# Last keys' scores of two head pairs in quarters of the array, and a pair's preparation two pairs ahead

## The chip, the core and the metric

The kernel runs on one core of a Trainium2 chip. A core has a matrix engine (TensorE, PE in the profile), a vector engine (VectorE, DVE), an activation engine (ScalarE, ACT), a general engine (GpSimd, POOL) and an engine that here only issues transfers (SyncE, SP). Each engine works through its own queue of instructions in order, and waits for others at semaphores. The metric is the device time of one execution in microseconds (us). Weight loads of the matrix engine are shown apart as PEld.

## The reference

Sigmoid attention over 8 batches of 12 heads, 448 tokens and 64 columns a head, and behind it a two-layer network with 2048 hidden columns on every token:

```python
def _attn_ref(q, k, v):                     # q, k, v: (8, 12, 448, 64), float32
    S = q.shape[2]
    scale = 1.0 / np.sqrt(q.shape[-1])
    scores = scale * np.matmul(q, k.transpose(0, 1, 3, 2)) - np.log(S)
    attn = 1.0 / (1.0 + np.exp(-scores))
    return np.matmul(attn, v).astype(np.float32)

def _moe_ref(x, w_in, w_out):               # x: (3584, 768), w_in: (768, 2048), w_out: (2048, 768)
    h = x @ w_in
    g = np.where(h > 0.0, h, np.exp(np.minimum(h, 0.0)) - 1.0)
    return (g @ w_out).astype(np.float32)
```

Between the two the heads are put side by side: x = attn_out.transpose(0, 2, 1, 3).reshape(3584, 768).

## The kernel before

**Numbers.** Matmuls run in float16. Each operand is a sum of a high and a low part (`split`, L135: ACT writes high, DVE writes low), and each product takes three matmuls: high by high, low by high, high by low. The scales that go with it are powers of two, found from the largest row sums (`mx` on DVE, a matmul `pr` that sums over the partitions, then a short chain on DVE and POOL up to `sc`).

**Pairs.** The unit of attention is a pair of heads: two heads of 64 columns lie on the two halves of the 128 rows of the array. A batch has NP = 6 pairs, numbered hp = 0 to 5. The 448 keys are cut in NC = 3 tiles of 128 and a rest of R = 64, the last keys. For each tile `scores` (L382) takes six matmuls of 448 columns into `psc`, on alternate row halves. For the last keys it takes six 64*64 matmuls, where the heads lie on the diagonal of the array and both write one bank of `psc`. `soften` (L397) takes the sigmoid on ACT (`sg`, L401) and splits it into `at` (ACT L430, DVE L431), for the last keys into `ar` (ACT L420, DVE L422). `values` (L436) multiplies with the values into `pav`, on alternate column halves, and `finish` splits the result into `xh`.

**Preparation of a pair** has three steps. `prepare` (L307) takes `mx` of the raw q, k and v. Its `scales` sends the matmul `pr` and makes `sc`. Its third step, `transposed`, splits q and k into `nat` and v into `vn` (ACT and DVE), and sends a transposing DMA (L362, on SP's queue) that turns `nat` into `qk`, what `scores` reads. The raw inputs come by DMAs on SP (`load_qk`, `load_v`), with two buffers each.

**Stages.** Batch 0 is computed in float32, while `w_in` is converted. Then its first layer runs (`moe1`: 16 tiles `ph` of 18 matmuls, exp and max into `g`) while `w_out` is loaded and converted (`load_w_out`, L217). The order of this first part is found by a scheduler, from the dependences. From batch 1 on, PE, ACT, DVE and SP run in the order of the code. Attention of batch b is woven with the second layer of batch b-1: `moe2` comes as steps of three matmuls (`po`, L550, 48 matmuls a tile), which `fill(n)` puts between the attention's matmuls. There are 96 steps beside batches 1, 3, 5 and 7, and 128 beside 2, 4 and 6, shared out evenly over the six pairs. After a batch's last pair, `rescale` (L464) brings its `xh` to one scale (DVE L471), and `moe1` of the batch runs.

**One pair's order** in the code is: scores and sigmoid and split of tiles 0 and 1; the third step of the next pair's preparation and the loads of the pair three ahead; 5 steps of `fill` (8 in a batch's first pair); `mx` of the pair after next; scores, sigmoid and split of tile 2 and of the last keys; the rest of the pair's `fill`; `pr` and the scales of the pair after next; `values`; `finish`. So a pair's `qk` is issued while the pair before it runs. `psc` has two buffers (of two banks each), `sg` four, `at` three, `ar` one, `qk` and `vn` two, `nat` one.

## Time and profile before

| | |
|---|---|
| median of 3 runs | 1238.27 us (1235.75 to 1238.64) |
| profiled execution | 1238.24 us, of it 1236.5 us span |
| mean granted clock of TensorE | 0.984 |
| batch 0, its first layer, conversion of the weights | to about 165 us |
| attention of batch 1 with moe2 of batch 0 | about 165 to 260 us |
| later batches: attention of 3 (96 steps) | 77 us between 468 and 545 us |
| moe1 of one batch, without a gap | 51.09 us for 270 of its 288 matmuls |

The span is what the profiler saw from the first to the last instruction; what lies around it is 1.7 us. The page has a line for each engine's busy time, a strip of 40 slices, the chain of work that ended last, and groups of instructions by line. In a timeline row stand the start and length in us, the engine, the line, the operation, the tiles written and read, the shape (rows*columns of the array for matmuls), the number of instructions, and, in brackets, how long the engine stood idle before and what ended that.

### The profile page before, as it was taken

Reading aid. Unit: us, or ns where it says so; the run is one execution under the profiler, and the core shown is the slowest. Engines: PE = TensorE matmul, PEld = TensorE weight load, DVE = VectorE, ACT = ScalarE, POOL = GpSimd, SP = SyncE. Lnnn points to the kernel's source line nnn. Section 1 sums busy time; section 2 is a strip of 40 time slices with the busy share of each in tenths; the row PEclk is TensorE's granted clock in tenths of the full one; section 3 lists DMA queues with packets and bytes.
Section 4 is the critical chain, followed back from the end, with each engine's and each line's share of the span. In section 5 each row is a group of like instructions: output and inputs, shape, how many; then the busy total and the mean of one; then the engine's idle time right before and its main releaser. Section 6 shows DMA issues by size and latency. Waiting matters only on the chain.

```text
span 1236.5 us, 19394 instructions
## 1 busy us (share of the span) xinstructions
PE 1170.5 (95%) x7342; PEld 605.9 (49%) x7342; DVE 828.8 (67%) x1742; ACT 725.2 (59%) x1099; POOL 71.8 (6%) x275
## 2 busy tenths in 40 slices
PE   5869878999999999999999999999999999999998
PEld 2324434545455554555555554545455554555565
DVE  5897988875677647885677646885577745875500
ACT  5866788853766337864666537764576435873300
POOL 1021000000000000100010000010000000100000
PEclk9989988999999999999999999999999999999999
DMA  8946423420134203440144202440044301420000
GB/s 223 284 127 193 142 80 86 110 70 1 45 90 97 52 1 69 112 90 1 25 102 98 60 1 46 110 109 7 1 94 99 91 1 23 112 44 7 1 26 26
DMA packets 219549, 91.32 MB, mean 74 GB/s; under 512 B 183616, under 2 KB 215360, under 8 KB 219456
## 3 DMA queue, kind: packets, MB, share of 16 engines
q1 hardware_dynamic: 219456, 90.09, 29.6%
q8 instruction: 57, 0.93, 0.3%
q14 instruction: 36, 0.29, 0.1%
HBM read 59.77 MB, written 11.01 MB: 57 GB/s over the span
## 4 chain that ended last, share of the span: by engine, by line
PE 78%; DVE 8%; ACT 7%; DMA 3%; issue 2%; SPq 1%; POOL 0%; DVEq 0%; ACTq 0%
PE ph L520 32%; PE po L550 26%; PE psc L390 8%; PE pav L453 7%; PE po_r L550 5%; ACT sg L401 2%; DMA stage<-in_moe_w_in_dram 2%; ACT at L430 1%; DVE mx L140 1%; DMA wo<-in_moe_w_out_dram 1%; ACT L401 1%; DVE at L431 1%; DVE nat L137 1%; DVE ar L422 1%; DVE e L535 1%
## 5 line engine op out<-in xcount | busy, mean ns | idle before, releaser
L520 PE MATMUL ph<-xh,wi 128*128 128x448 f16 x2304 | 443.5, 354 | 7.1 <-DVE xh L471 4.2
L550 PE MATMUL po<-wo,g 128*128 128x384 f16 x2304 | 392.7, 328 | 0.0
L550 PEld LDWEIGHTS <-g 128*128 128x128 f16 x2688 | 256.5, 98 | 197.5 <-issue 35.2
L520 PEld LDWEIGHTS <-wi 128*128 128x128 f16 x2304 | 225.7, 98 | 221.2 <-issue 11.1
L532 ACT ACTIVATE e<-ph,msc 128x448 f32<-128x448 f32 x128 | 80.9, 633 | 210.7 <-PE ph L520 210.6
L431 DVE SCALAR_TENSOR_TENSOR at<-sg,at 128x896 f16<-128x896 f32 x126 | 137.3, 1090 | 82.5 <-ACT at L430 82.5
L401 ACT ACTIVATE sg<-psc,bias,sc 128x896 f32<-128x896 f32 (+1 forms) x168 | 166.6, 992 | 1.5
L534 DVE TENSOR_SCALAR e<-e 128x448 f32<-128x448 f32 x128 | 50.3, 394 | 171.4 <-ACT e L532 171.4
L390 PE MATMUL psc<-qk 64*128 64x448 f16 x1008 | 117.8, 356 | 12.5 <-ACT sg L401 12.5
L430 ACT ACTIVATE at<-sg 128x896 f16<-128x896 f32 x126 | 119.6, 950 | 4.0
L136 ACT ACTIVATE xh<-pav,sc 128x448 f16<-128x448 f32 x48 | 30.4, 634 | 131.5 <-PE pav L453 129.8
L136 ACT ACTIVATE g<-e,msc 128x384 f16<-128x384 f32 (+1 forms) x192 | 95.9, 533 | 8.0 <-DVE e L535 5.7
L137 DVE SCALAR_TENSOR_TENSOR g<-e,msc,g 128x384 f16<-128x384 f32 (+1 forms) x192 | 94.6, 522 | 1.9 <-ACT g L136 1.5
L535 DVE SCALAR_TENSOR_TENSOR e<-ph,msc,e 128x448 f32<-128x448 f32 x128 | 87.5, 683 | 4.0
L390 PEld LDWEIGHTS <-qk 64*128 64x128 f16 x1008 | 41.9, 97 | 81.3 <-issue 58.9
L453 PE MATMUL pav<-at,vn 128*64 128x448 f16 x756 | 79.5, 355 | 0.0
L453 PEld LDWEIGHTS <-vn 128*64 128x64 f16 x924 | 48.8, 109 | 46.6 <-issue 18.5
L550 PE MATMUL po_r<-wo,g 128*128 128x384 f16 x384 | 64.8, 326 | 0.0
L334 POOL TENSOR_SCALAR sc<-pw 128x1 f32<-128x1 f32 x42 | 11.8, 281 | 833.1 <-DVE pw L103 632.1
L137 DVE SCALAR_TENSOR_TENSOR nat<-raw,sc,nat 128x384 f16<-128x384 f32 (+1 forms) x126 | 59.1, 523 | 0.0
L136 ACT ACTIVATE nat<-raw,sc 128x384 f16<-128x384 f32 (+1 forms) x126 | 58.8, 528 | 0.0
L558 DVE TENSOR_SCALAR o<-po,osc 128x384 f32<-128x384 f32 x48 | 29.6, 617 | 41.5 <-PE po L550 35.8
(105 smaller groups left out, 857.7 us busy)
## 6 DMA issues: line engine op xcount, KB each, us to landing
stage<-in_moe_w_in_dram SPq DMA_DIRECT2D x16, 768.0 KB, 6.6
raw<-in_q_dram SPq DMA_DIRECT2D x96, 96.0 KB, 3.2
raw<-in_k_dram SPq DMA_DIRECT2D x96, 96.0 KB, 2.8
rv<-in_v_dram SPq DMA_DIRECT2D x48, 192.0 KB, 2.8
out_dram<-o SPq DMA_DIRECT2D x48, 192.0 KB, 2.1
wo<-in_moe_w_out_dram SPq DMA_DIRECT2D x19, 384.0 KB, 3.9
so<-in_moe_w_out_dram SPq DMA_DIRECT2D x13, 384.0 KB, 4.1
rv<-in_v_dram SPq DMA_DIRECT2D x96, 32.0 KB, 2.5
```

Of the source, the lines that this page charges most:

```text
L136: nc.scalar.mul(hi, src, s)
L137: nc.vector.scalar_tensor_tensor(lo, src, s, hi, op0=ALU.mult, op1=ALU.subtract)
L390: nc.tensor.matmul(psc[:, j, :S] if g < NC else psc[rows[j], 0, :S], kk[rows[j], o], qq[rows[j], :S], start=(n == 0), stop=(n == len(parts ...
L401: a = nc.scalar.activation(sg[:, :nb], psc[:, :nb, :S], AF.Sigmoid, bias=bias, scale=self.s_scale)
L430: nc.scalar.mul(hi, sg, 2.0**ATOP)
L431: nc.vector.scalar_tensor_tensor(lo, sg, 2.0**ATOP, hi, op0=ALU.mult, op1=ALU.subtract)
L453: nc.tensor.matmul(pav[rows[j], :S], vv[i][:, 2 * NC + j if g == NC else j * NC + g], sg[k][:, j], start=(g == 0 and n == 0), stop=(g == N ...
L520: nc.tensor.matmul(ph[:, :S], wi[:, wj, c, f * P : (f + 1) * P], xh[:, c, xj], start=(n == 0), stop=(n == 3 * NK - 1),)
L532: a = nc.scalar.activation(e, ph[:, :S], AF.Exp, scale=inv)
L534: nc.vector.tensor_scalar(e, e, 1.0, -1.0, op0=ALU.min, op1=ALU.add)
L535: nc.vector.scalar_tensor_tensor(e, ph[:, :S], inv, e, op0=ALU.mult, op1=ALU.max)
L550: nc.tensor.matmul(po[:, :HM], lh(gj, f), wo[:, i, f, wj], start=(n == 0), stop=(n == 3 * NF - 1),)
```

## The change

The diff does six things.

1. **Last keys of two pairs at once.** A new function `last_keys` takes the last keys' scores of an even pair hp and of the odd pair hp + 1 together, right after the even pair's tile 0. It has three groups of four 64*64 matmuls, one for each quarter of the array. The two heads of the even pair lie on one diagonal of it, those of the odd pair on the other; each pair has a bank of its own in the tile `pscr`. Two sigmoids of 448 columns, one for each pair, write `sgr`. The odd pair's `ar` is split at the end of the even pair's fill.
2. **Order of scores.** An even pair has tile 0 and the last keys ahead of the first fill, tiles 1 and 2 behind it. An odd pair has tiles 0 and 1 ahead of it and tile 2 behind. `soften` is cut in `sigmoid` and `parts`, and where two tiles are taken in a row in the odd pair, both sigmoids stand ahead of both splits.
3. **Preparation two pairs ahead.** Pair n makes scales, `nat`, `vn` and `qk` of pair n + 2, and `mx` of pair n + 3. `scales` with its `pr` matmul moves from the end of the pair to a place behind the first two steps of fill, and the third step moves behind the late scores. `qk` and `vn` have three buffers, `sc` five, `ar` two.
4. **Batch ends.** A batch's first pair (but for batch 1) prepares nothing. The preparation of the next batch's third pair stands in `moe1`, at hidden tiles 3 and 5 (`beside`).
5. **Fill.** The first pair of a batch has two steps more than its even share, and 11 steps ahead of the late scores where it had 8. `xh` has one buffer instead of two.
6. **Ahead of batch 1** the whole preparation of its second pair, the `mx` of its third and the loads of its fourth are made, where before the scales of the second and the loads of the third were.

The diff, cut to its core:

```diff
-            sc = sb.tile([P, n + 3], F32, tag="sc", name=f"sc{u}", bufs=3)
+            sc = sb.tile([P, n + 3], F32, tag="sc", name=f"sc{u}", bufs=5)
...
-            qk = sb.tile([P, 2, 2 * NC + 1, P], F16, tag="qk", name=f"qk{u}", bufs=2)
+            qk = sb.tile([P, 2, 2 * NC + 1, P], F16, tag="qk", name=f"qk{u}", bufs=3)
...
-            vn = sb.tile([P, 2, 2 * NC + 2, D], F16, tag="vn", name=f"vn{u}", bufs=2)
+            vn = sb.tile([P, 2, 2 * NC + 2, D], F16, tag="vn", name=f"vn{u}", bufs=3)
...
+        def soften(self, g):
+            nb = 2 if g < NC else 1
+            psc = self.psc.pop(g)
+            sg = sb.tile([P, 2, S], F32, tag="sg", name=f"sg{g}{self.u}", bufs=SB)
+            self.sigmoid(sg[:, :nb], psc[:, :nb, :S])
+            self.sg[g] = [sg]
+
+        def parts(self, g):
+
             if g == NC:
-                ar = sb.tile([P, 2, S], F16, tag="ar", name=f"ar{self.u}")
-                for j, r in enumerate(rows):
-                    nc.scalar.mul(ar[r, j], sg[r, 0], 2.0**ATOP)
+                (sg, i) = self.sg[g]
+                ar = sb.tile([P, 2, S], F16, tag="ar", name=f"ar{self.u}", bufs=2)
+                of = [rows[j ^ i] for j in range(2)]
+                for j, r in enumerate(of):
+                    nc.scalar.mul(ar[r, j], sg[r, i], 2.0**ATOP)
...
+    def last_keys(two):
+
+        psc = ps.tile([P, 2, 512], F32, tag="psc", name=f"pscr{two[0].u}", bufs=2)
+        o = slice(S, S + R)
+        for n in range(3):
+            for i, p in enumerate(two):
+                hi, lo = p.qk
+                kk, qq = [(hi, hi), (lo, hi), (hi, lo)][n]
+                for j in range(2):
+                    nc.tensor.matmul(
+                        psc[rows[j ^ i], i, :S], kk[rows[j], o], qq[rows[j], :S],
+                        start=(n == 0), stop=(n == 2),
+                    )
+        sg = sb.tile([P, 2, S], F32, tag="sg", name=f"sgr{two[0].u}", bufs=SB)
+        for i, p in enumerate(two):
+            p.sg[NC] = [sg, i]
+
+        def soften():
+            for i, p in enumerate(two):
+                p.sigmoid(sg[:, i], psc[:, i, :S])
+
+        return soften
...
-            xh_of[b] = sb.tile([P, NK, 2, S], F16, tag="xh", name=f"xh{b}", bufs=2)
...
     def pair_of(n):
         b, hp = pairs[n]
+        if hp == 0:
+            xh_of[b] = sb.tile([P, NK, 2, S], F16, tag="xh", name=f"xh{b}")
...
-    third = prepare_pair(EXACT * NP + 1)()
+    prepare_pair(EXACT * NP + 1)()()
     load_pair(EXACT * NP + 2)
+    load_pair(EXACT * NP + 3)
+    scales = prepare_pair(EXACT * NP + 2)
+    prepared = EXACT * NP + 2
...
+    def prepare_next():
+        nonlocal prepared, scales
+        load_pair(prepared + 2)
+        prepared += 1
+        scales = prepare_pair(prepared)
+
+    def beside(f):
+        nonlocal third
+        if f == 3:
+            third = scales()
+        if f == 5:
+            third()
+            prepare_next()
...
-                share = left // (NP - hp)
+                share = left // (NP - hp) + (2 if hp == 0 else 0)
                 tail = 4 if hp == NP - 1 else 0
-                p = pair_of(n)
-                for t in range(2):
+                works = hp > 0 or b == EXACT
+                if hp == 0:
+                    two = pair_of(b * NP), pair_of(b * NP + 1)
+                elif hp % 2 == 0:
+                    two = pair_of(b * NP + hp), pair_of(b * NP + hp + 1)
+                p = two[hp % 2]
+                p.scores(0)
+                if hp % 2 == 0:
+                    soften = last_keys(two)
+                    p.soften(0)
+                    soften()
+                    p.parts(0)
+                    early_ones, late_ones = (0,), (1, 2)
+                else:
+                    p.scores(1)
+                    p.soften(0)
+                    p.soften(1)
+                    p.parts(0)
+                    p.parts(1)
+                    early_ones, late_ones = (0, 1), (2,)
+
+                gap = 11 if hp == 0 else 5
+                fill(2)
+                if works:
+                    third = scales()
+                fill(gap - 2)
+                for t in late_ones:
                     p.scores(t)
+                for t in late_ones:
                     p.soften(t)
-                third()
...
+                    p.parts(t)
+                if hp % 2 == 0:
+                    p.parts(NC)
+                if works:
+                    third()
+                    prepare_next()
...
                 if hp == NP - 1:
-                    h = hidden(b)
+                    h = hidden(b, beside if b + 1 < B else None)
                     next(h)
                 fill(share - gap - tail)
-                third = second()
+                if hp % 2 == 0:
+                    two[1].parts(NC)
                 for t in range(NC + 1):
                     p.values(t)
                 p.finish()
```

Three places show what this does to the queues. The first is ACT's queue in the second pair (hp 1) of batch 2. `sg` is a sigmoid, `at` and `ar` are high parts of the sigmoids, `nat` and `vn` high parts of a later pair's q, k and v; the figure behind the tile's name is the pair or the key tile's pair. Before:

```order
L401 ACTIVATE sg_1_3276<-psc_1_3269,bias,sc_1_2592 128x896
L430 ACTIVATE at_1_3278<-sg_1_3276 128x896
L401 ACTIVATE sg_1_3288<-psc_1_3281,bias,sc_1_2592 128x896
L430 ACTIVATE at_1_3290<-sg_1_3288 128x896
L136 ACTIVATE nat_2_3293<-raw_2_2500,sc_2_3234 128x384
L136 ACTIVATE nat_2_3293<-raw_2_2500,sc_2_3234 128x128
L136 ACTIVATE nat_2_3293<-raw_2_2500,sc_2_3234 128x384
L136 ACTIVATE vn_2_3302<-rv_85,sc_2_3234 128x512
L401 ACTIVATE sg_1_3342<-psc_1_3335,bias,sc_1_2592 128x896
L430 ACTIVATE at_1_3344<-sg_1_3342 128x896
L401 ACTIVATE sg_1_3354<-psc_1_3347,bias,sc_1_2592 128x448
L420 ACTIVATE ar_1_3356<-sg_1_3354 64x448 x2
```

and now:

```order
L398 ACTIVATE sg_1_3322<-psc_1_3308,bias,sc_1_2535 128x896
L398 ACTIVATE sg_1_3324<-psc_1_3315,bias,sc_1_2535 128x896
L434 ACTIVATE at_1_3326<-sg_1_3322 128x896
L434 ACTIVATE at_1_3329<-sg_1_3324 128x896
L398 ACTIVATE sg_1_3369<-psc_1_3362,bias,sc_1_2535 128x896
L434 ACTIVATE at_1_3371<-sg_1_3369 128x896
L136 ACTIVATE nat_3_3374<-raw_3_2577,sc_3_3344 128x384
L136 ACTIVATE nat_3_3374<-raw_3_2577,sc_3_3344 128x128
L136 ACTIVATE nat_3_3374<-raw_3_2577,sc_3_3344 128x384
L136 ACTIVATE vn_3_3383<-rv_86,sc_3_3344 128x512
L136 ACTIVATE xh_3145<-pav_1_3453,sc_1_2535 128x448
```

The splits of `nat` and `vn` stand behind all three sigmoids and splits instead of behind two of them, and they are those of pair 3, not of pair 2. The sigmoid and `ar` of the last keys have left this pair.

The second place is DVE's queue in the third pair (hp 2) of batch 2, from its first split on. Before:

```order
L431 SCALAR_TENSOR_TENSOR at_2_3463<-sg_2_3461,at_2_3463 128x896
L431 SCALAR_TENSOR_TENSOR at_2_3475<-sg_2_3473,at_2_3475 128x896
L137 SCALAR_TENSOR_TENSOR nat_3_3478<-raw_3_3119,sc_3_3419,nat_3_3478 128x384
L137 SCALAR_TENSOR_TENSOR nat_3_3478<-raw_3_3119,sc_3_3419,nat_3_3478 128x128
L137 SCALAR_TENSOR_TENSOR nat_3_3478<-raw_3_3119,sc_3_3419,nat_3_3478 128x384
L137 SCALAR_TENSOR_TENSOR vn_3_3487<-rv_86,sc_3_3419,vn_3_3487 128x512
L140 TENSOR_REDUCE mx_4_3515<-rv_85 128x4
L140 TENSOR_REDUCE mx_4_3515<-raw_4_3305 128x7
L318 TENSOR_TENSOR mx_4_3515<-mx_4_3515,half 128x2
L431 SCALAR_TENSOR_TENSOR at_2_3529<-sg_2_3527,at_2_3529 128x896
L422 SCALAR_TENSOR_TENSOR ar_2_3541<-sg_2_3539,ar_2_3541 64x448 x2
L558 TENSOR_SCALAR o_2_0_3549<-po_2_0_3382,osc_1591 128x384
```

and now, from its second split on:

```order
L435 SCALAR_TENSOR_TENSOR at_2_3557<-sg_2_3555,at_2_3557 128x896
L435 SCALAR_TENSOR_TENSOR at_2_3562<-sg_2_3560,at_2_3562 128x896
L425 SCALAR_TENSOR_TENSOR ar_2_3565<-sgr_2_3499,ar_2_3565 64x448 x2
L137 SCALAR_TENSOR_TENSOR nat_4_3570<-raw_4_2858,sc_4_3519,nat_4_3570 128x384
L137 SCALAR_TENSOR_TENSOR nat_4_3570<-raw_4_2858,sc_4_3519,nat_4_3570 128x128
L137 SCALAR_TENSOR_TENSOR nat_4_3570<-raw_4_2858,sc_4_3519,nat_4_3570 128x384
L137 SCALAR_TENSOR_TENSOR vn_4_3579<-rv_85,sc_4_3519,vn_4_3579 128x512
L140 TENSOR_REDUCE mx_5_3592<-rv_86 128x4
L140 TENSOR_REDUCE mx_5_3592<-raw_5_3386 128x7
L318 TENSOR_TENSOR mx_5_3592<-mx_5_3592,half 128x2
L585 TENSOR_SCALAR o_r_3642<-po_r_3537,osc_1617 128x384
L425 SCALAR_TENSOR_TENSOR ar_3_3650<-sgr_2_3499,ar_3_3650 64x448 x2
```

All three splits of `at` and the pair's `ar` now stand ahead of `nat`, `vn` and `mx`, and a second `ar`, the odd pair's, behind them and behind the output tile `o`.

The third place is SP's queue around 100 us, ahead of the loads of `w_out` (L241), where `raw` and `rv` are loads of a pair's q, k and v. Before:

```order
L362 DMA_TRANSPOSE qk_0_805<-nat_0_798 128x14x128
L268 DMA raw_2_885<-in_q_dram 128x3x64 x2
L272 DMA raw_2_885<-in_q_dram 64x2x64
L268 DMA raw_2_885<-in_k_dram 128x3x64 x2
L272 DMA raw_2_885<-in_k_dram 64x2x64
L241 DMA wo<-in_moe_w_out_dram 128x384 x8
L241 DMA so_2_1346<-in_moe_w_out_dram 128x384
L241 DMA so_4_1383<-in_moe_w_out_dram 128x384
```

and now:

```order
L268 DMA raw_2_896<-in_q_dram 128x3x64 x2
L272 DMA raw_2_896<-in_q_dram 64x2x64
L268 DMA raw_2_896<-in_k_dram 128x3x64 x2
L272 DMA raw_2_896<-in_k_dram 64x2x64
L362 DMA_TRANSPOSE qk_1_891<-nat_1_884 128x14x128
L268 DMA raw_3_906<-in_q_dram 128x3x64 x2
L272 DMA raw_3_906<-in_q_dram 64x2x64
L268 DMA raw_3_906<-in_k_dram 128x3x64 x2
L272 DMA raw_3_906<-in_k_dram 64x2x64
L280 DMA rv_86<-in_v_dram 128x2x192
L285 DMA rv_86<-in_v_dram 64x2x64 x2
L241 DMA wo<-in_moe_w_out_dram 128x384 x8
```

A second transposing DMA and the loads of a further pair stand between the loads of `raw_2` and the first loads of `w_out`.

More of the change, by code (lines that the diff above doesn't have):

```diff
@@ L395, in scores, with sigmoid @@
             self.psc[g] = psc
-        def soften(self, g):
-            b, nb = self.b, 2 if g < NC else 1
-            psc = self.psc.pop(g)
-            sg = sb.tile([P, 2, S], F32, tag="sg", name=f"sg{g}{self.u}", bufs=SB)
-            a = nc.scalar.activation(
-                sg[:, :nb], psc[:, :nb, :S], AF.Sigmoid, bias=bias, scale=self.s_scale
-            )
-            if b - 1 in last_exp:
+        def sigmoid(self, to, psc):
+            a = nc.scalar.activation(to, psc, AF.Sigmoid, bias=bias, scale=self.s_scale)
+            if self.b - 1 in last_exp:
                 tc.add_manual_dep(
                     a.ins,
-                    last_exp[b - 1],
+                    last_exp[self.b - 1],
                     mybir.DependencyInfo(
@@ L412, in soften @@
                 )
-            if b < EXACT:
-                self.sg[g] = [sg]
-                return
-            if g == NC:
-                ar = sb.tile([P, 2, S], F16, tag="ar", name=f"ar{self.u}")
-                for j, r in enumerate(rows):
-                    nc.scalar.mul(ar[r, j], sg[r, 0], 2.0**ATOP)
-                for j, r in enumerate(rows):
+        def soften(self, g):
[5 more added lines that the diff above has]
+        def parts(self, g):
+            if g == NC:
+                (sg, i) = self.sg[g]
[3 more added lines that the diff above has]
+                    nc.scalar.mul(ar[r, j], sg[r, i], 2.0**ATOP)
+                for j, r in enumerate(of):
                     nc.vector.scalar_tensor_tensor(
-                        ar[rows[1 - j], j], sg[r, 0], 2.0**ATOP, ar[r, j],
+                        ar[of[1 - j], j], sg[r, i], 2.0**ATOP, ar[r, j],
                         op0=ALU.mult, op1=ALU.subtract,
@@ L427, in soften @@
                 return
+            (sg,) = self.sg[g]
             at = sb.tile([P, 2, 2, S], F16, tag="at", name=f"at{g}{self.u}", bufs=AB)
@@ L701, in attention_ffn @@
     of_moe2 = next(h)
+    def prepare_next():
[10 more added lines that the diff above has]
+            prepare_next()
+    third = None
     E = mybir.EngineType
@@ L718, in attention_ffn @@
             for hp in range(NP):
-                n = b * NP + hp
-                share = left // (NP - hp)
+                share = left // (NP - hp) + (2 if hp == 0 else 0)
                 tail = 4 if hp == NP - 1 else 0
-                p = pair_of(n)
-                for t in range(2):
+                works = hp > 0 or b == EXACT
[24 more added lines that the diff above has]
+                for t in late_ones:
                     p.scores(t)
+                for t in late_ones:
                     p.soften(t)
-                third()
-                if n + 3 < len(pairs):
-                    loaded[n + 3] = load_qk(*pairs[n + 3]), load_v(*pairs[n + 3])
-                gap = 8 if hp == 0 else 5
-                fill(gap)
-                second = prepare_pair(n + 2)
-                for t in range(2, NC + 1):
-                    p.scores(t)
-                    p.soften(t)
+                    p.parts(t)
[4 more added lines that the diff above has]
+                    prepare_next()
                 if b == EXACT and hp < NC:
```

## The prediction

> **What bounds the kernel now.** The page's first part gives each engine's busy time and its share of the span:
>
> ```profile
> PE 1170.5 (95%) x7342; PEld 605.9 (49%) x7342; DVE 828.8 (67%) x1742; ACT 725.2 (59%) x1099; POOL 71.8 (6%) x275
> ```
>
> TensorE is the bound, and the other two have room on average. An average hides stages, so I cut the span into stages (windows view; busy time of PE, PEld, DVE, ACT, POOL, then the clock). The first row is the expert layer after batch 2, the second the attention of batch 3:
>
> ```profile
> 408.00:468.00 60.00, 60.00 (x334) 30.95 (x331) 32.09 (x72) 20.86 (x34) 2.33 (x9) 1.00 0.06 16
> 468.00:545.00 77.00, 73.53 (x541) 38.32 (x539) 62.95 (x119) 62.38 (x85) 5.76 (x26) 1.00 0.45 99
> ```
>
> The expert layer has no gap, and the change leaves its matmuls alone. In attention PE stands idle for 3.5 of 77 us while DVE and ACT are over 80% busy. So the change can be worth two things: PE slots in attention, and the waits there. The waits of PE after 250 us (waits view: total, times, longest) are mostly these two:
>
> ```profile
> PE psc L390 <- ACT sg L401: 6.7, 6, 1.2
> PE pr L128 <- DVE mx L318: 6.6, 6, 1.1
> ```
>
> One ordinary pair of batch 3, PE's timeline (start, length, instructions):
>
> ```profile
> 519.88 1.31 PE L390 MATMUL psc<-qk 64*128 64x448 f16 x12
> 521.12 2.61 PE L550 MATMUL po<-wo,g 128*128 128x384 f16 x15
> 523.66 1.43 PE L390 MATMUL psc<-qk 64*128 64x448 f16 x12
> 525.02 5.54 PE L550 MATMUL po<-wo,g 128*128 128x384 f16 x33
> 530.39 0.17 PE L128 MATMUL pr<-mx,ones 128*128 128x12 bf16 x1
> 530.50 1.89 PE L453 MATMUL pav<-at,vn 128*64 128x448 f16 x18
> 532.22 0.55 PE L453 MATMUL pav<-ar,vn 128*64 128x448 f16 x4
> 532.70 1.31 PE L390 MATMUL psc<-qk 64*128 64x448 f16 x12
> 414.72 51.09 PE ph L520 x270
> ```
>
> The last row (chain of waits) sets the price of a 448-column slot: 51.09/270 = 0.189 us. The first twelve score matmuls take 521.12-519.88 = 1.24, that is six slots (1.135) and one change of the array's shape (0.105): two matmuls on the two halves of the rows share a slot. The second dozen holds the last keys' six 64*64 matmuls and takes 1.36: six slots and two changes. A pair lasts 12.82 us, without a wait. po's period is (5.37-0.10)/33, about 0.16. With 128 moe2 steps (batches 2, 4, 6) a pair has five or six steps more and lasts about 15.3.
>
> **Part 1, the quarters.** Two pairs spend six slots and two changes on last keys now. Afterwards, if four 64*64 quarters share a slot, three slots and one change: 3 x 0.189 + 0.10 = 0.66 us per two pairs, 21 times two pairs, **-13.9 us** (-1.98 a batch). If a quarter group takes two slots, 0.567 x 21 = 11.9 of it is lost. No row shows four at once, so the ends are 2 and 13.9. I take 13.9: two row halves into two banks, two column halves with different right sides (pav L453, 18 in 530.50 to 532.22, nine slots), and two quarters of one diagonal into one bank (the dozen at 523.66) all run side by side already.
>
> On that last point stands a rule against the change: the Trainium skill, page "TensorEngine Tiling (Array Packing)", section "Restrictions and Gotchas", says that different row tiles cannot use one PSUM bank at the same time. Each group of four puts both row halves into each bank. By the rule the sum would be 11.9 higher; but the old diagonal breaks it too and takes one slot in the trace, so it only gets a part of that rival's chance.
>
> **Part 2, waits that go.** Starts of a batch with 96 steps (470 on) and with 128 (324):
>
> ```profile
> 472.75 0.76 PE L390 MATMUL psc<-qk 64*64 64x448 f16 x6 [1.03 <-ACT sg L401]
> 478.64 0.17 PE L128 MATMUL pr<-mx,ones 128*128 128x12 bf16 x1 [1.13 <-DVE mx L318]
> 324.47 0.76 PE L390 MATMUL psc<-qk 64*64 64x448 f16 x6 [1.22 <-ACT sg L401]
> 542.49 0.17 PE L128 MATMUL pr<-mx,ones 128*128 128x12 bf16 x1 [1.06 <-DVE mx L318]
> 468.34 1.28 ACT L401 ACT_TABLE_LOAD   x1
> ```
>
> Behind the table load the first sigmoids come about 4 us after the first scores. In the first pair 33 po matmuls (5.4 us) now stand ahead of the second scores instead of 24, and its preparation is gone; both waits of that place go. With the short shape changes beside them (0.06 to 0.16 each, and 0.29 on ar) I count 4.28 us of waits in batches 3 and 5, 2.77 in batch 7 (no wait in its last pair), 1.28 in batches 2, 4 and 6, and 1.5 in batch 1 behind its start.
>
> **Part 3, waits that come.** ACT and DVE of the same ordinary pair, in the old order (T = 519.88):
>
> ```profile
> 520.66 1.10 ACT L401 ACTIVATE sg<-psc,bias,sc 128x896 f32<-128x896 f32 x1
> 524.62 1.40 ACT L136 ACTIVATE nat<-raw,sc 128x384 f16<-128x384 f32 x3
> 528.50 0.71 ACT L401 ACTIVATE sg<-psc,bias,sc 128x448 f32<-128x448 f32 x1
> 529.24 1.17 ACT L420 ACTIVATE ar<-sg 64x448 f16<-64x448 f32 x2
> 525.75 1.40 DVE L137 SCALAR_TENSOR_TENSOR nat<-raw,sc,nat 128x384 f16<-128x384 f32 x3
> 527.07 0.75 DVE L137 SCALAR_TENSOR_TENSOR vn<-rv,sc,vn 128x512 f16<-128x512 f32 x1
> 528.33 1.08 DVE L140 TENSOR_REDUCE mx<-raw 128x7 bf16<-128x896 f32 x1
> 530.64 1.27 DVE L422 SCALAR_TENSOR_TENSOR ar<-sg,ar 64x448 f16<-64x448 f32 x2
> DMA to landing us min/median/max: 4.0/4.0/4.4
> ```
>
> From T+0.78 ACT does sg, at, sg, at at 0.99 each and reaches nat at T+4.74; DVE ends nat at T+7.27, and the transposing DMA (last row) lands it 4.0 later, T+11.3. In the new odd pair a third sigmoid and split stand ahead: nat is 1.98 later, so it ends at about T+9.25 and **lands at T+13.3**. Formerly a whole pair lay between landing and use; now the next even pair's quarters want it right after its first scores. The second pair (15 steps) lasts 12.82 - 0.69 - 0.49 = 11.64, and six matmuls with a change are 0.67: wanted at T+12.3. So the third pair's quarters **wait 1.0**. In batches 2, 4 and 6 it is wanted at about T+15.2, and nothing waits.
>
> The quarters stand in PE's queue ahead of po, so the whole queue waits. In the third pair ACT has two short sigmoids (2 x 0.71) more ahead of its splits, so it reaches ar at 0.78 + 6 x 0.99 + 2 x 0.71 = T+8.1; ar, nat, vn, mx (0.68 + 1.08 + 0.17), o and the second ar then keep DVE until about T+16, 3.5 past the pair's end. The fourth pair's splits start some 1 us late on DVE, with at, at, the scale chain (1.03) and at ahead of nat: landing at about T+14.45 against 12.8 wanted, **1.65** in the fifth pair. The last pair has nat, vn and mx ahead of the rescaling of xh:
>
> ```profile
> 545.26 2.12 PE L550 MATMUL po<-wo,g 128*128 128x384 f16 x12
> 547.22 3.57 PE L520 MATMUL ph<-xh,wi 128*128 128x448 f16 x18
> 545.03 1.90 DVE L471 TENSOR_SCALAR xh<-xh,rr 128x896 f16<-128x896 f16 x5
> ```
>
> The first rescaled part is now ready at about T+12.4 with an idle DVE, T+14 with that lag, and ph wants it at T+12.13: 0.3 to 1.9. I take 1.9, since DVE's queue is filled, with 0.45 and 0.35 for the scale and pb around it. The first pair takes its 3 x 0.99 splits and two ars behind two more short sigmoids: pav waits about 0.95 for ar. The fourth pair's scale: 0 to 0.9, taken 0.3. Sum for batches 3 and 5: 0.95 + 1.0 + 0.3 + 1.65 + 2.7 = 6.6. Against 4.28 + 1.98 this is **+0.35 each**. Batch 7 prepares nothing at its end: 3.9 - 2.77 - 1.98 = **-0.85**. Batches 2, 4 and 6: -1.28 - 1.98 = **-3.26 each**.
>
> **Part 4, batch 1 and what is ahead of it.** SP's rows and DVE by stretch (windows):
>
> ```profile
> 99.98 1.24 SPq L285 DMA_DIRECT2D rv<-in_v_dram  x2
> 101.27 1.69 SPq L362 DMA_TRANSPOSE qk<-nat  x1
> 103.01 1.83 SPq L268 DMA_DIRECT2D raw<-in_q_dram  x2
> 107.59 4.48 SPq L241 DMA_DIRECT2D wo<-in_moe_w_out_dram  x8
> 102.20:107.20 5.00, 5.00 (x28) 2.60 (x27) 3.46 (x11) 2.51 (x4) 0.82 (x4) 1.00 0.73 148
> 107.20:112.20 5.00, 5.00 (x27) 2.39 (x26) 1.80 (x5) 1.72 (x4) 0.00 (x0) 1.00 0.86 221
> 112.20:119.50 7.30, 6.93 (x37) 3.11 (x36) 5.72 (x12) 6.43 (x14) 0.00 (x0) 1.00 1.02 395
> 176.53 0.48 PE L165 MATMUL so<-wo,ones 128*128 128x384 bf16 x1 [6.45 <-DVE wo L158]
> 197.02 1.30 PE L390 MATMUL psc<-qk 64*128 64x448 f16 x6 [4.22 <-ACT sg L401]
> ```
>
> A second transposing DMA (1.7) and the loads of a further pair's q, k (107.59 - 103.01 = 4.6) and v (1.24 and a third load, some 1.7) now stand ahead of the first w_out loads, so these start up to 8 later, and DVE, which bounds their conversion until 176, with them. DVE's idle time from 102 to 119.5 is 1.54 + 3.20 + 1.58 = 6.3, which takes the moved nat, vn, mx and scale chain (5.0). The delay lies between 0 and 8; I take 2.6. In batch 1 DVE also carries the rest of w_out, so the wait in the third pair lies between 1.0 and 1.0 + 4.2 (the row's wait): 3.8, in the fifth 2.5, at the end 2.7. With -1.5 and -1.98 this is +5.5, in all **+8.1**.
>
> **Sum:** -9.8 + 0.7 - 0.85 + 8.1 = -1.9 on the profiled execution's 1238.24 (the median is 1238.27): **1236.4 us**, no change; 0.3%, about what a measurement of this kernel can tell, is 3.7 us.
>
> **Rivals.** (a) **The waits for qk are shorter.** If the chain nat, transposing DMA, quarters is 1 us quicker than summed, because ACT runs ahead of DVE where I queued them, the waits of third and fifth pairs lose 2 in each of four batches: 1228. For it speaks the room on both engines, against it that every link is a row. Without any delay in batch 1: 1222. (b) **Slower: the chain is later.** Each us more costs 2 in each short batch, 8 in all; beyond 1.9 the long batches wait too. From 0.7 on the time is over 1242; at 1.0 it is 1244.4, at 1.5 about 1248. For it speaks that DVE is 82% busy in that stage and nat stands behind three more of its instructions. (c) **The quarters don't run four at once**, so the change doesn't do what it says: 1236.4 + 11.9 = 1248.
>
> **How the numbers follow.** The forecast, with its own range 1232 to 1242, has 0.36, (a) 0.36, (b) 0.18, (c) 0.10. Faster by over 0.3% (under 1234.5): 0.33 from (a) and 0.08 from the forecast's lower part, 0.41. Slower (over 1242): 0.14 from (b), 0.09 from (c), 0.23. The rest, 0.36, is within 0.3%. A range of 1225 to 1248 leaves out about 0.09 on either side.
>
> **What would show it.** Right: twelve 64*64 matmuls in about 0.6 us; no wait of psc for ACT in the first pairs; in batches 3 and 5 the third and fifth pairs' quarters wait 1 to 2 us behind the transposing DMA, with none in 2, 4 and 6; ph waits for xh; w_out loads start later. Wrong: quarters in 1.1 us, waits for qk in long batches or in none, or a stage that the sum leaves alone (the expert layer) longer than 51.09 per 270.

## The result and the profile after

| | before | changed |
|---|---|---|
| median | 1238.19 us (4 runs, 1235.75 to 1238.64) | 1247.13 us (4 runs, 1245.96 to 1248.09) |
| ratio to before | | 1.0076, 95% interval 1.0058 to 1.0093 |
| profiled execution | 1238.24 us | 1246.27 us |

The change makes the kernel slower by 0.8%, where no change was forecast. The engines' line of the page of the changed kernel:

```profile
PE 1162.9 (93%) x7342; PEld 599.5 (48%) x7342; DVE 828.8 (67%) x1742; ACT 722.4 (58%) x1099; POOL 95.2 (8%) x275
```

PE has 7.6 us less to do, and the span is longer: the saving is real and the waits outgrow it. To see where, the program is cut at its hidden layers (`ph`). An attention stage lasts from the last hidden matmul of one layer to the first of the next:

| stage | before | changed | forecast | measured |
|---|---|---|---|---|
| start of the program to the layer of batch 1 | 262.6 | 275.4 | +8.1 | +12.8 |
| attention of batches 2, 4, 6 | 3 x 94.1 | 90.9, 90.9, 91.1 | -9.8 | -9.5 |
| attention of batches 3 and 5 | 2 x 81.8 | 2 x 83.5 | +0.7 | +3.5 |
| attention of batch 7 | 80.1 | 81.0 | -0.85 | +0.9 |
| the layers of batches 1 to 7 | 7 x 54.35 | 3 x 54.52, 4 x 54.37 | 0 | +0.6 |
| sum | | | -1.9 | +8.3 |

The two profiled executions differ by 8.0; the rest is rounding and the program's end.

PE's timeline of the changed kernel in batch 3, the quarters and their neighbours:

```profile
475.43 0.74 PE L390 MATMUL psc<-qk 64*128 64x448 f16 x6
476.11 0.76 PE L477 MATMUL pscr<-qk 64*64 64x448 f16 x12
476.80 5.54 PE L577 MATMUL po<-wo,g 128*128 128x384 f16 x33
...
502.39 0.38 PE L477 MATMUL pscr<-qk 64*64 64x448 f16 x2
504.15 0.76 PE L477 MATMUL pscr<-qk 64*64 64x448 f16 x10 [1.38 <-DMA qk<-nat]
...
529.21 0.38 PE L477 MATMUL pscr<-qk 64*64 64x448 f16 x2
531.87 0.76 PE L477 MATMUL pscr<-qk 64*64 64x448 f16 x10 [2.29 <-DMA qk<-nat]
...
558.70 3.56 PE L547 MATMUL ph<-xh,wi 128*128 128x448 f16 x18 [2.25 <-DVE xh L498]
```

Twelve quarters take 476.80 - 476.11 = 0.69 us, three slots and a change: four run at once. In the third and fifth pairs the first two, on the even pair's own `qk`, start at once; the next needs the odd pair's `qk`, and PE stands for its transposing DMA. The two take a slot that four could share, and the ten behind the wait take 504.84 - 504.15 = 0.69 us, as twelve do. So the whole stretch from 502.39 to 504.15 is lost, 1.76 us, and 2.66 in the fifth pair. (The expectation of the quarters' experiment below takes a slot off each, 1.57 and 2.47.)

Why the `qk` is late stands in the odd pair ahead of it (hp 1 of batch 3), first in ACT's timeline, then in DVE's and POOL's:

```profile
495.77 0.95 ACT L434 ACTIVATE at<-sg 128x896 f16<-128x896 f32 x1
497.97 1.41 ACT L136 ACTIVATE nat<-raw,sc 128x384 f16<-128x384 f32 x3 [1.24 <-POOL sc L329]
```

```profile
493.79 2.09 DVE L435 SCALAR_TENSOR_TENSOR at<-sg,at 128x896 f16<-128x896 f32 x2 [1.07 <-ACT at L434]
496.41 0.17 DVE L328 RECIPROCAL sc<-pw 128x3 f32<-128x3 f32 x1
496.76 1.09 DVE L435 SCALAR_TENSOR_TENSOR at<-sg,at 128x896 f16<-128x896 f32 x1
498.62 1.42 DVE L137 SCALAR_TENSOR_TENSOR nat<-raw,sc,nat 128x384 f16<-128x384 f32 x3 [0.77 <-ACT nat L136]
```

```profile
496.89 1.05 POOL L329 TENSOR_SCALAR sc<-sc 128x3 f32<-128x3 f32 x1
```

ACT is ready for `nat` at 496.7, but `sc` isn't there. Its chain stands behind two splits of `at` on DVE (493.79) and leaves DVE at 496.6, and then POOL's step takes 1.05 us, beside DVE's third split of `at`. In the even pair, with DVE idle, the same step takes 0.23.

```profile
509.25 0.23 POOL L329 TENSOR_SCALAR sc<-sc 128x3 f32<-128x3 f32 x1
```

Over the whole execution POOL's 275 instructions take 95.2 us, where they took 71.8. The waits view of the whole execution has ACT's wait 19 times, the third row; it was in no list before, where the scales were made a pair earlier:

```profile
PE pscr L477 <- DMA qk<-nat: 14.8, 8, 2.8
PE ph L547 <- DVE xh L498: 11.0, 4, 4.2
ACT nat L136 <- POOL sc L329: 27.8, 19, 2.6
```

The start. SP's, ACT's, DVE's and PE's timelines of the changed kernel: the first loads of w_out, the first work on them, and the last matmul on w_out's magnitudes (`so`); the last row is that matmul in the kernel before:

```profile
106.91 1.53 SPq L362 DMA_TRANSPOSE qk<-nat  x1
114.97 4.68 SPq L241 DMA_DIRECT2D wo<-in_moe_w_out_dram  x8
```

```profile
119.26 0.55 ACT L153 ACTIVATE wo<-wo 128x384 f32<-128x384 f32 x1 [4.23 <-DMA wo<-in_moe_w_out_dram]
120.27 0.56 DVE L158 SCALAR_TENSOR_TENSOR wo<-wo 128x384 uint32<-128x384 uint32 x1 [4.02 <-ACT wo L157]
```

```profile
187.04 0.48 PE L165 MATMUL so<-to,ones 128*128 128x384 bf16 x1 [0.30 <-DVE to L158]
```

```profile
178.70 0.48 PE L165 MATMUL so<-to,ones 128*128 128x384 bf16 x1 [0.69 <-DVE to L158]
```

The loads start 7.4 us later than at 107.59, and the conversion ends 8.3 later. (Here and below, `so` ends where its last matmul starts, and a pair where its last matmul into `pav` starts.) The second pair of batch 1 ends at 218.0 instead of 209.4, 8.6 later. On ACT's queue behind `so` lie the last splits of w_out, in turn with DVE's, and that pair's first sigmoids come only behind them:

```profile
200.39 1.15 ACT L136 ACTIVATE wo<-wo,swo 128x384 f16<-128x384 f32 x2 [1.92 <-DVE wo L137]
204.29 1.15 ACT L136 ACTIVATE wo<-wo,swo 128x384 f16<-128x384 f32 x2 [0.15 <-DVE wo L137]
207.05 2.07 ACT L398 ACTIVATE sg<-psc,bias,sc 128x896 f32<-128x896 f32 x2
```

### The profile page after: what moved, and what is told of

Its sections match the earlier page's. It is cut to its first block, busy times and chain, and to the rows that moved or that the text cites. A ratio compares the mean times of both kernels' runs of the same rounds, so it can differ in the third digit from the quotient of the medians.

```text
span 1244.5 us, 19369 instructions
## 1 busy us (share of the span) xinstructions
PE 1162.9 (93%) x7342; PEld 599.5 (48%) x7342; DVE 828.8 (67%) x1742; ACT 722.4 (58%) x1099; POOL 95.2 (8%) x275
## 4 chain that ended last, share of the span: by engine, by line
PE 69%; DVE 12%; ACT 7%; DMA 6%; issue 2%; SPq 2%; POOL 1%; DVEq 0%; ACTq 0%
PE ph L547 31%; PE po L577 22%; PE po_r L577 5%; PE pav L457 5%; PE psc L390 5%; DMA qk<-nat 3%; ACT sg L398 2%; DVE at L435 2%; DMA stage<-in_moe_w_in_dram 2%; DVE mx L140 2%; DVE nat L137 1%; DVE ar L425 1%; PE pscr L477 1%; ACT at L434 1%; DMA wo<-in_moe_w_out_dram 1%
## 5 line engine op out<-in xcount | busy, mean ns | idle before, releaser
L398 ACT ACTIVATE sg<-psc,bias,sc 128x896 f32<-128x896 f32 x126 | 135.5, 1092 | 18.9 <-PE psc L390 16.7
L390 PE MATMUL psc<-qk 64*128 64x448 f16 x756 | 87.4, 353 | 4.1 <-ACT sg L398 4.1
L457 PE MATMUL pav<-at,vn 128*64 128x448 f16 x756 | 80.3, 358 | 0.0
L390 PEld LDWEIGHTS <-qk 64*128 64x128 f16 x756 | 30.2, 94 | 52.8 <-issue 33.9
```

The lines of the kernel that those rows point to most:

```text
L390: nc.tensor.matmul(psc[:, j, :S] if g < NC else psc[rows[j], 0, :S], kk[rows[j], o], qq[rows[j], :S], start=(n == 0), stop=(n == len(parts ...
L398: a = nc.scalar.activation(to, psc, AF.Sigmoid, bias=bias, scale=self.s_scale)
L457: nc.tensor.matmul(pav[rows[j], :S], vv[i][:, 2 * NC + j if g == NC else j * NC + g], sg[k][:, j], start=(g == 0 and n == 0), stop=(g == N ...
```

## The experiments

All are edits of the changed kernel or of one built on it. The time before, on the chips of these runs, had medians of 1236.1 to 1236.7 us, where it was 1238.2 beside the changed kernel's 1247.13. So differences from the changed kernel are uncertain by some 2 us, and the ratios to the time before on the same chip decide.

### The loads of batch 1's fourth pair behind eight w_out loads

```diff
-    load_pair(EXACT * NP + 3)
...
         if f >= 2:
             step(W_OUT)
+        if f == 8:
+            load_pair(EXACT * NP + 3)
```

> Edit to the changed kernel (1247.1): the loads of the fourth pair of batch 1 are issued behind the first eight w_out loads instead of ahead of them. Theory A (SP's queue: the first w_out load is issued at 114.97 instead of 107.59, DVE then stands idle 4.0 us in 116 to 120): these loads start about 6.5 us earlier, the first layer of batch 0 (80.3 us, 73.4 before) shortens by 4 to 6 us, and the time is 1241 to 1243. Theory B (DVE is bound by the moved work, nat, vn, mx and the scale chain of two pairs, 5 us): the loads start earlier, but the layer shortens by 1.5 us at most: 1245.6 or more.

1246.06 us (1245.20 to 1251.49), ratio 1.0090, interval 1.0067 to 1.0112. The first layer of batch 0 fell from 80.3 to 73.9 us, as by A, but the time hardly moved, as by B. `so` ends at 184.3 instead of 187.0 and the second pair at 215.8: of the 6.4 us that the layer gained, 2.2 are left behind the conversion. So it isn't the layer's length that sets the end there; the end of the conversion fits better. The profiled execution is the longest of the four, with a low granted clock behind several waits (last section).

### The quarters behind the first fill

```diff
-                if hp % 2 == 0:
-                    soften = last_keys(two)
-                    p.soften(0)
-                    soften()
-                    p.parts(0)
-                    early_ones, late_ones = (0,), (1, 2)
-                else:
-                    p.scores(1)
...
+                p.scores(1)
...
+                late_ones = (2,)
...
+                if hp % 2 == 0:
+                    soften = last_keys(two)
                 for t in late_ones:
                     p.scores(t)
+                if hp % 2 == 0:
+                    soften()
```

> Edit to the changed kernel (1247.1): an even pair takes tiles 0 and 1 ahead of its first fill, as an odd pair does, and the quarters and tile 2 behind it, 2.5 us or more later on PE. Theory A (the quarters stand in PE's queue ahead of everything and wait for the transposing DMA: 1.57 and 2.47 us of lost time in each of batches 3, 5 and 7, 1.24 and 2.98 in batch 1): all these waits go, 3 x 4.0 + 4.2 = 16 us, 1231; batches 2, 4 and 6 stay at 90.87. Theory B (the wait is only moved: ar comes later and pav waits for it, or DVE is so full that the pair's end waits instead): a quarter to a half of it comes back as waits of pav on ar, 1235 to 1240. Theory C (the lost time is not these waits): 1246 or more.

1222.08 us (1221.78 to 1222.40), ratio 0.9887, interval 0.9872 to 0.9901: some 23 us under the changed kernel by the two ratios (25 by the medians), more than A's 16. PE's timeline in the third pair of batch 3, and the waits view behind 250 us:

```profile
494.92 1.31 PE L390 MATMUL psc<-qk 64*128 64x448 f16 x12
496.16 1.15 PE L577 MATMUL po<-wo,g 128*128 128x384 f16 x6
497.15 0.17 PE L128 MATMUL pr<-mx,ones 128*128 128x12 bf16 x1
497.18 1.62 PE L577 MATMUL po<-wo,g 128*128 128x384 f16 x9
498.73 0.76 PE L477 MATMUL pscr<-qk 64*64 64x448 f16 x12
499.42 0.74 PE L390 MATMUL psc<-qk 64*128 64x448 f16 x6
```

```profile
PE ph L547 <- DVE xh L498: 4.5, 3, 1.5
PE pscr L477 <- DMA qk<-nat: 0.6, 1, 0.6
```

The quarters stand 3.1 us later and run without a gap; po is done meanwhile. Batch 3 fell from 83.55 to 76.94, batch 7 from 80.95 to 75.24, batches 2 and 4 stayed at 90.87. Batch 3 lost 4.42 us to the quarters' two waits and 6.6 are gone: 4.4 in the third and fifth pairs, and the rest in the others, where pav's wait for `ar` (first pair) and pr's (fourth) went as well and ph's fell from 2.25 to 1.49. Theories B and C fall. But the edit also takes the even pair's tile 1 ahead of the fill, and no run parts this from the place of the quarters: what is shown is the worth of the new order.

### mx behind the rescaling

```diff
                     third()
-                    prepare_next()
+                    if hp < NP - 1:
+                        prepare_next()
...
                     h = hidden(b, beside if b + 1 < B else None)
                     next(h)
+                    prepare_next()
```

> Edit to the changed kernel (1247.1): in a batch's last pair mx of the next pair (1.93 us of DVE) comes behind the rescaling of xh instead of ahead of it. Theory A (ph waits 2.25 us for DVE's rescaling in batches 1, 3 and 5): the wait falls to about 0.4 there, three times 1.9: 1241.4. Theory B (mx is then late for its pr in the next layer, which stands in PE's queue at hidden tile 3, or xh's own split is late): nothing gained, 1246 to 1248.

1247.82 us (1245.29 to 1252.84), ratio 1.0108, interval 1.0079 to 1.0136: nothing gained. PE and DVE at the layer of batch 3:

```profile
555.98 3.19 PE L547 MATMUL ph<-xh,wi 128*128 128x448 f16 x16 [0.46 <-DVE xh L498]
559.89 0.54 PE L547 MATMUL ph<-xh,wi 128*128 128x448 f16 x2 [0.72 <-DVE xh L137]
561.33 0.22 PE L114 MATMUL pb<-dg,ones 128*128 128x128 bf16 x1 [0.90 <-DVE dg L110]
```

```profile
557.97 1.08 DVE L140 TENSOR_REDUCE mx<-raw 128x7 bf16<-128x896 f32 x1
559.16 0.68 DVE L137 SCALAR_TENSOR_TENSOR xh<-pav,sc,xh 128x448 f16<-128x448 f32 x1
```

The attention of batch 3 is 1.7 shorter and its layer 1.8 longer. `mx` now holds up the last pair's own split of xh and, behind it, `dg`: theory B, in its second form.

### The scale chain ahead of the splits

```diff
                     p.soften(1)
-                    p.parts(0)
-                    p.parts(1)
...
                 if works:
                     third = scales()
+                if hp % 2:
+                    p.parts(0)
+                    p.parts(1)
```

> Edit to the changed kernel (1247.1): in odd pairs the scale chain (al, al, pw, sc, xs, xs) stands ahead of the two splits of at on DVE instead of behind them. ACT waits for POOL's sc ahead of nat in every odd pair (1.24, 2.62, 2.62 in batch 3). Theory A (this wait is the link that the sum left out): ACT no longer waits for sc, nat's low part starts 0.77 earlier on DVE (its idle time there), and the waits of the quarters and of ph fall by 0.8 each: batch 3 by 2.3, four batches 8 to 9 us, 1238 to 1239. Theory B (DVE's queue is the limit, not sc): the splits of at are moved behind by the same 1.0 and nat ends where it did: 1246 or more.

1244.39 us (1239.11 to 1246.42), ratio 1.0057, interval 1.0035 to 1.0079. That overlaps the changed kernel's 1.0058 to 1.0093, so the medians alone show no gain. In batch 3 the quarters' waits fell from 1.38 and 2.29 to 0.55 and 1.78, ph's from 2.25 to 1.70, close to A. But the stage is only 0.27 shorter in this execution, where these three falls make 1.9. PE's timeline in the fifth pair, the window there, and POOL's and ACT's timelines:

```profile
530.51 1.11 PE L477 MATMUL pscr<-qk 64*64 64x448 f16 x10 [1.78 <-DMA qk<-nat]
531.55 2.10 PE L577 MATMUL po<-wo,g 128*128 128x384 f16 x6
```

```profile
532.00:536.00 4.00, 4.00 (x24) 1.91 (x23) 1.69 (x5) 1.84 (x3) 0.34 (x2) 0.73 0.49 116
```

```profile
493.98 1.92 POOL L332 COPY sc<-sc 64x1 f32<-64x1 f32 x2
```

```profile
524.78 0.91 ACT L136 ACTIVATE nat<-raw,sc 128x128 f16<-128x128 f32 x2 [1.35 <-POOL sc L332]
```

The first three rows: behind the wait six po take 1.9 us instead of 0.98, at a granted clock of 0.73 (windows view). From the wait's end to the next scores 4.88 us pass (530.51 to 535.39), where it was 3.26 (531.87 to 535.13): these 1.6 us are what the stage didn't gain. The runs say the same: their time goes with the mean granted clock of each, from 1239.11 us at 0.982, near A's time, to 1246.42 at 0.975; the changed kernel's four runs had 0.981 to 0.985. The last two rows: POOL's other steps now stand beside DVE's splits of `at` and take 1.92 instead of 0.40, and ACT waits for these in the fourth pair. The step of 1.05 us, now beside an idle DVE, takes 0.23 here (at 493.69). So `sc` is a link of the late chain: freeing it took 0.83 off the third pair's wait and 0.51 off the fifth's. A holds for the waits; the time doesn't part the two theories.

### One pair's last keys at a time

```diff
-                if hp % 2 == 0:
-                    soften = last_keys(two)
+                soften = last_keys((p,))
...
-                if hp % 2 == 0:
-                    two[1].parts(NC)
```

> Edit to e2_quarters_later (1222.1): every pair takes its own last keys, six 64*64 matmuls on one diagonal of the array in three slots, in the place where e2 has the quarters of two pairs. All else of the change stays. Theory A (four quarters share a slot, 0.66 us for two pairs, 21 times): 1222.1 + 13.9 = 1236. Theory B (the gain of e2 comes from the order and the preparation ahead alone, and the quarters only spread the same work): 1222 to 1225.

1233.06 us (10 runs, 1231.72 to 1235.02), ratio 0.9974, interval 0.9964 to 0.9983: 11.0 over the kernel with quarters, against 13.9 of A and at most 3 of B. Batches 2, 4 and 6 are 92.9 instead of 90.87, 2.04 each; batch 5 is only 0.9 longer; the short wait for `qk` that it had with quarters (0.6) is gone. The quarters are worth what their slots cost, where nothing waits.

### mx in the next layer

```diff
         nonlocal third
+        if f == 0:
+            prepare_next()
         if f == 3:
```

with `prepare_next` left out in a batch's last pair.

> Edit to e2_quarters_later (1222.1): mx of the next batch's third pair moves from the last pair into the next layer, behind hidden tile 0. Theory A (in e2 ph still waits 1.5 to 2.3 us for the rescaling in batches 1, 3 and 5, and the run e3_rescale_first gave the gain back only because mx then stood ahead of xh's own split and of dg): the wait goes without a new one, 1.5 to 2.2 each: 1216 to 1218. Theory B (whatever is moved in DVE's queue there comes back as a wait for dg or xh): 1221 to 1223.

1217.19 us (1215.87 to 1219.63), ratio 0.9850, interval 0.9833 to 0.9867: 4.9 less, theory A. ph and pb of batch 3's layer no longer wait:

```profile
541.61 2.12 PE L577 MATMUL po<-wo,g 128*128 128x384 f16 x12
543.57 3.57 PE L547 MATMUL ph<-xh,wi 128*128 128x448 f16 x18
546.99 0.22 PE L114 MATMUL pb<-dg,ones 128*128 128x128 bf16 x1
```

### The loads behind ten w_out loads, and both together

```diff
         if f == NF - 1:
             step(1)
+            load_pair(EXACT * NP + 3)
...
-    load_pair(EXACT * NP + 3)
```

> Edit to e2_quarters_later (1222.1): the loads of the fourth pair of batch 1 are issued behind the first ten w_out loads, where those wait for free buffers. In e1_loads_later they stood behind eight, and the ninth was issued at 122.1 (112.2 before the change), so that a part of the delay stayed. Theory A (the order of SP's queue makes the delay): the last w_out tile is through 3 us or more earlier than in e1, and the time falls by 4 to 6: 1216 to 1218. Theory B (the end of w_out's conversion is bound by its own chain of three buffers and by the moved work, and batch 1 starts as late as before): 1220 to 1222.

1219.53 us (1218.29 to 1221.82), ratio 0.9869, interval 0.9854 to 0.9884: 2.5 less, between A and B. `so` ends at 183.6 (185.8 in the kernel that it was made from), the second pair at 215.0 (216.8).

> e2_quarters_later with the edits of e6_mx_in_layer and e7_loads_last together. Theory A of both: the gains lie in different stages and add up, 1211 to 1214. Theory B of both: 1220 to 1222.

**1213.22 us** (1212.37 to 1213.43), ratio 0.9815, interval 0.9800 to 0.9829: the two add up, theory A, and this beats both kernels: 1.85% under before's 1236.1 on the same chip, some 2.6% under the changed kernel by the two ratios. Behind 250 us PE waits for one thing only:

```profile
PE pscr L477 <- DMA qk<-nat: 0.5, 1, 0.5
```

### What keeps the start late

> Edit to e8_both (1213.2): in the first two pairs of batch 1 the low parts of the sigmoids' splits are left out (the high part stands in their place as matmul operand), six DVE instructions of 1.09 us less, 6.5 us of DVE; the matmuls and all other instructions stay. It asks what still keeps the end of batch 1's second pair at 213.1 where it was 209.4 before the change. Theory A (DVE's work ahead of the third pair sets it: preparation two pairs ahead puts one more nat, vn, mx and scale chain, 5.1 us, ahead of that point): the pair ends 5 to 6.5 earlier, 1207 to 1209. Theory B (the end of w_out's conversion sets it, a chain from DMA to ACT to DVE to PE through three buffers, and the moved work lies beside it): 2 us at most, 1211 or more.

The edit returns `[hi, hi]` ahead of DVE's split where `self.b == EXACT and self.hp < 2`; this kernel leaves out those low parts, so it serves for the time alone. 1211.33 us (1210.74 to 1211.77), ratio 0.9799, interval 0.9784 to 0.9813. 6.5 us of DVE give 1.9, and the second pair ends at 212.2 instead of 213.1: B, that work on DVE alone doesn't set this point.

> Edit to e8_both (1213.2): in the second pair of batch 1 alone, pr and its scale chain stand behind tile 2's scores instead of behind the first six po. There pr waits 3.8 us for DVE's mx with po, scores and values queued behind it on PE, and 4.1 us later scores wait for a sigmoid. Theory A (DVE and ACT set the end of this pair, so the two waits only fill time in which PE has no other work): 1212 to 1214. Theory B (PE's queue is stopped by pr, and po behind it could have run): 2 to 4 us less, 1209 to 1211.

1215.11 us (1214.00 to 1218.15), ratio 0.9838, interval 0.9820 to 0.9855, 1.9 more: the second pair ends at 213.5, so nothing was won by letting po pass, and B falls; the forecast of A (1212 to 1214) is missed by 1 us on the slow side.

> Edit to e8_both (1213.2): ahead of batch 1 only what was made before the change is made (the scales of the second pair, the loads of the third). The second pair's nat, vn and transposing DMA, the third pair's mx and scales and the fourth's loads go into batch 1's first pair, behind its first two splits. In every run so far the end of batch 1's second pair lies 30.4 to 31.7 us behind the last so matmul of w_out's conversion (178.7 before the change, 187.0 with it, 182.7 in e8). Theory A (the conversion's end sets the start of batch 1, and what stands ahead of its loads and beside it delays it): the last so comes at 178 to 180, the second pair ends 2.5 to 4 earlier, 1209.5 to 1211. Theory B (the moved work only returns in the first pair, where nat, the transposing DMA and the quarters are now in one chain): the last so is earlier, but the second pair ends at 213 or later, 1213 to 1216.

```diff
-    prepare_pair(EXACT * NP + 1)()()
+    second = prepare_pair(EXACT * NP + 1)()
     load_pair(EXACT * NP + 2)
...
+                first = b == EXACT and hp == 0
+                if first:
+                    second()
+                    two[1] = pair_of(b * NP + 1)
+                    load_pair(b * NP + 3)
+                    scales = prepare_pair(b * NP + 2)
```

1216.34 us (1215.45 to 1216.67), ratio 0.9836, interval 0.9819 to 0.9852, 3.1 more. PE's timeline:

```profile
179.20 0.48 PE L165 MATMUL so<-to,ones 128*128 128x384 bf16 x1 [0.59 <-DVE to L158]
188.08 1.33 PE L477 MATMUL pscr<-qk 64*64 64x448 f16 x10 [8.41 <-DMA qk<-nat]
```

`so` ends at 179.2, half a microsecond from before the change: what stood ahead of w_out's loads and beside its conversion was nearly all of that delay. But the quarters of the first pair then wait 8.4 us for `qk`, and the second pair ends at 214.9. That is B for the time (0.3 above its range) and A for the cause of the conversion's delay.

In e11 that pair ends 35.7 us behind the last `so`, and in e9 28.6. In before, changed, e1 to e8 and e10 the second pair of batch 1 ends 30.4 to 31.7 us behind the last `so`.

## Why the forecast was wrong

- **Part 1, the quarters: right.** Twelve take 0.69 us, and -1.98 a batch fits batches 2, 4 and 6, forecast at -3.26 and measured at -3.25 twice and -3.0. With nothing waiting, 21 times two pairs are worth 11.0 (e5 against e2), 13.0 in the profiled executions, against 13.9. The rule of the Trainium skill, page "TensorEngine Tiling (Array Packing)", section "Restrictions and Gotchas", that row tiles cannot share a PSUM bank at one time, is not what the trace shows.
- **Part 2, the waits that go: right.** Behind 320 us, in batches 2 to 7, the changed kernel's list of PE's waits has no psc waiting for a sigmoid; pr waits for mx three times, 0.4 each, and in the fourth pair, not in the first or last.
- **Part 3, the waits that come: right place, mis-sized.** Both quarters' waits were forecast, at 1.0 and 1.65; they cost 1.76 and 2.66, together 1.8 more. Batches 3 and 5 are each 1.4 off and batch 7 1.7, so that the smaller terms nearly cancel. The step that failed is "nat is 1.98 later": it let ACT reach `nat` behind its own queue and left out that `nat` also needs `sc`, whose chain the change had moved behind two splits of `at` on DVE, and whose POOL step takes 1.05 there instead of 0.23. (For the fifth pair the chain on DVE was counted, but not POOL's step.) With the odd pair's start at T = 490.05, DVE ends `nat` at T + 10.0 and not at T + 9.25, and `qk` lands at T + 14.06 and not at T + 13.3, which is the third pair's 0.76. The Trainium skill, page "SBUF — State Buffer", section "SBUF: two separate sides", says that a DVE operation with two SBUF inputs and a GpSimd operation that reads SBUF lock each other out for a whole instruction. The trace agrees: `at`'s split reads two tiles in SBUF, and POOL's step ends 0.09 us behind it. Experiment e4 moved the chain and took 0.83 and 0.51 off the two waits: all of the third pair's excess, half of the fifth's 1.01, whose other half stays open. The wait of ph was forecast at 1.9 and measured at 2.25. That of pav for `ar` in the first pair was forecast at 0.95 and cost about 0.8: that pair lasts 14.62 us here and 13.82 in e2, which has no such wait.
- **Part 4, the start: mis-sized.** The delay of w_out's conversion was bounded by 0 and 8 and taken at 2.6, since DVE's idle time would take the moved work. That step failed: the delay was 8.3, the upper end. By the end of `so` two things made it, about half each: it is 185.8 to 187.9 in the six kernels with the fourth pair's loads ahead of w_out's (changed, e2 to e6), 182.3 to 183.6 in the four with them behind (e7 to e10), and 179.2 in e11, which has no early preparation either. DVE stood idle for the late loads (4.02 at 120.27, by way of ACT), and the moved preparation cost the conversion some 3.8 us although DVE had idle time; why, the runs don't show. Behind it the third pair's wait in batch 1 cost 1.43 and not 3.8, the fifth's 3.17 and not 2.5. The sum of the stage was +12.8 against +8.1.
- **Rivals.** The measured time lies where rival (b) put it, from 1 us of lateness on 1244 to 1248, and that is in part luck. Its mechanism was at work, the later chain in short batches (0.76 and 1.01 more than forecast), but it gives about half of the 10.2 us that the sum was off; the other half came from the start, which no rival priced beyond the range of Part 4. (a) falls, and (c), at 1248 close to the measured time, falls by the 0.69 us.
- **What the forecast didn't see**: the same operations in another order lose very little. The order of e2 is worth 23 us: each of the quarters' waits held up all that is queued behind it on PE, while 2.4 us of po that were ready stood there.

What stays open: e7 and e8 have `so` still 4 to 5 us later than before. e11 shows that this delay goes with the early preparation of two pairs, but not which of its instructions (the transposing DMA ahead of the loads, `nat` and `vn`, or `mx`) makes it.

## What to carry to other kernels

When an operand is asked for earlier than before, write down its whole chain with every engine in it, small scale steps too, and put the reader behind work that is ready: here an order with twelve matmuls behind fifteen others turned 0.8% slower into 1.1% faster. When an operation is moved within a queue to end a wait, look at what then stands behind it: the wait can come back there (e3 against e6). A range that is wide for one term needs a reason for the value taken in it; that an engine has idle time there doesn't show that moved work is free (Part 4).

## What the runs showed of the hardware

- **A wait can cost more than its length.** Behind a wait of 2.79 us in e1 the granted clock was 0.59 for 5 us, and behind 1.78 in e4 0.73 for 4. e1 has three more such stretches (0.50 to 0.58, behind waits of 2.25, 2.30 and 2.26), e4 two more (0.57 and 0.66, behind 2.31 and 1.75), the changed kernel none between 215 and 1200 us: behind the waits of 1.38 and 2.29 in the changed kernel's batch 3, and behind one of 2.79 in its batch 1, it stayed at 1.00. Behind waits of over 4 us it was low in both kernels: 0.50 from 200 to 209 in the changed one (waits of 4.46 and 4.10), 0.50 from 197 to 202 before (4.22). e1's window (the columns as before, the clock third from the end):

```profile
248.00:253.00 5.00, 5.00 (x23) 2.26 (x23) 1.85 (x6) 1.76 (x3) 1.22 (x6) 0.59 0.46 125
```

  Between runs e1, e3 and e4 scatter by 6 to 8 us, the changed kernel by 2, and those without these waits (e2, e6 to e8) by 0.6 to 4. In e1, e3 and e4 the longest run has the lowest mean granted clock, 0.975 to 0.978, against 0.982 or 0.983 of the shortest, so the scatter goes with the clock; why it falls in one run and not in another is left open. The Trainium skill, page "TensorE: Matmul & The Clock Gate", section "HAM oscillation — how this bites in real kernels", warns of idle gaps over about 3.4 us; those of over 4 us fit that, and those in e1 and e4 were shorter.
- **Small POOL steps beside DVE's splits** of `at` take four to five times their time: 1.05 for 0.23, and 1.92 for 0.40 for two copies.
- Four 64*64 matmuls in the four quarters of the array run at once, with each pair of diagonal quarters on one bank: 0.69 us for twelve of 448 columns.
